# Attention kernel with two concatenated parts: reordered start-up (GpSimd work, weight and transposing loads, keep matmuls) and a halved last step

## Chip, cores, metric

One core of a Trainium2 chip. In the profile's lines PE is TensorE (matrix products), DVE VectorE, ACT ScalarE (the exponentials), POOL or Pool GpSimd and SP SyncE; a name with q, as ACTq, is that engine issuing a load or store. The granted clock is the share of full speed that the profile's records give for PE's clock; a keep matmul is one on zeros whose only use is to keep PE busy. The time of a run is device microseconds of that core; the span of a profile is about 2 us shorter than the time of the same run. A ratio between two kernels is the mean time of one kernel's runs over the mean time of the other's runs of the same rounds. The rounds of the experiments ran on four chips of the same kind, and the kernel before was run again in each of them; where medians of different rounds are compared, the text says so.

## The reference

Two attention blocks on sequences of 2048 rows, width 448, 16 heads of 28, both in bf16; their outputs are concatenated.

```python
# A: plain multi-head attention
qkv = x @ wqkv;  scores = q @ k.T * 28 ** -0.5
a = (softmax(scores) @ v) @ wo
# B: four segments of 512 rows, causal attention inside a segment, plus a memory
#    of the earlier segments (phi = elu + 1), gated by sigmoid(beta)
p = softmax(qs @ ks.T * scale + mask);  a_dot = p @ vs
a_mem = (phi(qs) @ M) / (phi(qs) @ z + 1e-6)
o = g * a_mem + (1 - g) * a_dot;  M += phi(ks).T @ vs;  z += phi(ks).sum()
b = o @ wo
return concatenate([a, b], -1)
```

## The kernel before

Names: P = 128, CW = 512 rows to a block, GW = 112 = four heads of 28, HP = 32 (a head padded to 32), D = 448. `xn` is the first block of A's input as rows, `xT` the input transposed, `wpad` the k or q weights with every head padded to 32 columns, `w["0"]` a small tile with the first four heads' weights, `w["A"]` the full weights of A (the profile calls it wstA).

```python
nc.sync.dma_start(out=xn[:], in_=Ax[0:CW, :]...)            # SP queue, 448 KB
load_w("0", A_wqkv, GW, D, GW, nc.scalar)                   # small k weights, ACT queue
load_w("0", A_wqkv, 0, 0, GW, nc.gpsimd)                    # small q weights, Pool queue
# ... Pool: memsets of wpad, vA, vB, woA, woB, phik, mblk, masks, one after the other ...
keep(11)                                                    # matmuls on zeros, while xn is on its way
# 16 transposes of xn on PE -> PSUM -> xT["A", 0, 0..3] (two copies by DVE, two by ACT)
for which in ("q", "k"):                                    # the padded copies, on DVE
    nc.vector.tensor_copy(out=wpad[which, "A"]...[:, :, 0:4, 0:DH], in_=w["0"]...)
nc.vector.memset(w["A"][KC // 2:KC // 2 + 1, 3, 0:2], 0.0)  # holds the next load until here
load_w("A", A_wqkv, 0, 0, 3 * D, nc.scalar)                 # 1008 KB + 168 KB, ACT queue
for r in (1, 2, 3):                                         # rows 512 to 2047, held until here
    for c in range(NKC):
        load_xT("A", Ax, r, c, nc.sync, hold if r == 1 and c == 0 else None)
# 8 matmuls: first projections of k and q -> kT by DVE, qT by ACT; 3 keep matmuls
```

`load_w` makes two loads: 384 rows in one, the last 64 rows in the other. After this comes a software pipeline of 395 units: three score matmuls into PSUM, one exponential over 128x1536 on ACT, three matmuls with v. Everything else on PE (projections, v, outputs) is put between the units as filler. v of the first four heads (`g_v0`) takes its weights from `w["A"]`.

After the last unit comes a chain for the last block:

```python
nc.vector.reciprocal(rc[:], pd[:])
nc.vector.tensor_copy(out=rb..., in_=rc...to_broadcast(...))   # 128x512
# 4 fp32 matmuls -> pb (128x512);  oT = o * pb on DVE;  4 output matmuls (t = 0..3)
# casts: t = 0, 2 on DVE, stored from SP; t = 1, 3 on ACT, stored from ACT
```

The softmax here doesn't subtract the row's maximum and nothing guards it: scores larger than these inputs give would overflow.

## Time and profile before

Median 586.03 us of four runs (585.21 to 587.72).

| stage of the profiled run (585.21 us) | us |
|---|---|
| start to first exponential | 16.14 |
| first exponential to end of the last | 554.02 |
| last exponential to end | 12.84 |

From the page: busy time of the engines as a share of the span, PE's granted clock in 40 slices (9 is 90% or more of full speed), and the group of exponentials (output and input, count, then busy us, mean ns, and after the bar idle us before them).

```profile
...
PE 519.6 (89%) x3869; PEld 172.4 (30%) x3912; DVE 200.4 (34%) x386; ACT 548.9 (94%) x427; POOL 21.2 (4%) x41
...
PEclk8899999999999999999999999999999999999999
...
L448 ACT ACTIVATE pt<-ps_s 128x1536 bf16<-128x1536 f32 x395 | 538.7, 1590 | 10.3 <-PE ps_s L444 5.4
...
```

ACT is 94% busy and nearly all of it is exponentials with 10.3 us of idle time before them in total: the middle is bound by ACT. Only the first two slices, up to about 29 us, show PE's clock below 90%. So the ramp and the tail are what can be shortened, and a microsecond won in the ramp moves the whole train of exponentials.

The timeline of the first 24 us (start, duration, engine, line, operation, how many; in brackets the idle time of the engine before it and what ended it):

```profile
...
6.77 0.97 POOL L132 MEMSET vB<- 128x1024 bf16 x1
...
7.13 0.74 DVE L274 COPY wpqA<-w 128x448 bf16<-128x448 bf16 x1
...
7.79 2.85 DVE L274 COPY wpkA<-w 128x448 bf16<-128x448 bf16 x1
...
8.62 1.90 POOL L161 MEMSET woA<- 128x1792 bf16 x1
...
10.79 1.01 PE L290 MATMUL ps_h<-xTA,wpkA 128*128 128x512 bf16 x2 [3.93 <-DVE wstA L281]
...
12.08 0.49 ACTq L110 DMA_DIRECT2D wstA<-in_A_wqkv_dram  x1
...
16.14 1.45 ACT L448 ACTIVATE pt<-ps_s 128x1536 bf16<-128x1536 f32 x1 [1.15 <-PE ps_s L435]
17.25 0.41 PE L224 MATMUL ps_v<-wstA,xTA 128*128 128x112 bf16 x5 [0.91 <-DMA wstA<-in_A_wqkv_dram]
...
18.03 2.79 ACT L448 ACTIVATE pt<-ps_s 128x1536 bf16<-128x1536 f32 x2 [0.44 <-PE ps_s L435]
...
21.89 3.02 ACT L448 ACTIVATE pt<-ps_s 128x1536 bf16<-128x1536 f32 x2 [1.07 <-PE ps_s L435]
...
```

The two padded copies on DVE have the same shape, but one lasts 0.74 and the other 2.85 us, while Pool's memsets run beside it (two of them, of vB and woA, are shown). The q copy ends at 7.87 us, and the k copy at 10.64 us. The first projection waits for them until 10.79 us. The second part of the full weight load is issued at 12.08 us, and PE waits for it in the middle of v (17.25 us). Then the second exponential is 0.44 us late, and the fourth 1.07 us.

By stage (busy us of each engine, then PE's clock, DMA share and GB/s):

```profile
...
core 0: us, PE busy (x) PEld busy (x) DVE busy (x) ACT busy (x) POOL busy (x), PEclk, DMA share, GB/s
0.00:16.14 16.14, 10.91 (x44) 4.20 (x45) 5.43 (x10) 3.15 (x6) 14.82 (x24) 0.79 0.64 154
16.14:21.89 5.75, 4.35 (x34) 1.57 (x32) 0.62 (x1) 4.24 (x3) 4.51 (x15) 0.77 1.13 156
21.89:570.20 548.31, 497.72 (x3756) 162.91 (x3797) 190.26 (x368) 540.48 (x417) 1.83 (x3) 1.00 0.15 37
570.20:583.00 12.80, 6.62 (x41) 3.67 (x40) 4.11 (x8) 1.06 (x2) 0.00 (x0) 0.98 0.16 54
...
```

The clock is 0.79 and 0.77 of full speed in the first two stages and 1.00 in the middle. (The DMA share exceeds 1 in this view, 1.13 in the second stage; nothing here rests on that column.) The tail in the timeline:

```profile
...
577.03 0.69 DVE L639 TENSOR_TENSOR oT<-osb,ps_b 128x512 bf16<-128x512 f32 x1 [1.33 <-PE ps_b L636]
...
577.78 0.93 PE L591 MATMUL ps_yl<-woA,oT 128*128 128x448 bf16 x4 [0.78 <-DVE oT L639]
...
579.31 0.36 ACTq L602 DMA_DIRECT2D out_dram<-y  x1
579.87 0.53 ACT L597 CAST y<-ps_yl 128x448 bf16<-128x448 f32 x1 [0.59 <-DVE y L599]
580.43 0.36 ACTq L602 DMA_DIRECT2D out_dram<-y  x1
```

The multiply over 128x512 takes 0.69 us, and only then come the four output matmuls. ACT's second cast starts 0.59 us after its first has ended, because ACT issues a store in between (the bracket names DVE, but that cast had ended at 579.53 us, and the store's issue ended at 579.67); the span ends 2.2 us after the last issue.

### The profile page before, as it was taken

What the parts mean: (1) busy time and instruction counts of PE and PEld (TensorE: products, weight loads), DVE (VectorE), ACT (ScalarE), POOL (GpSimd) and SP (SyncE); (2) the same over time, 40 slices, a digit from 0 to 9 for tenths busy, and PEclk for the clock granted to TensorE, in tenths of its full rate; (3) what the DMA queues carried; (4) which work ended last, traced back from release to release, by engine and by line L of the source; (5) the groups of instructions that cost most, each with busy time, mean ns of one, the idle gap of its engine ahead of it and who ended that gap; (6) DMA issues with size and microseconds to landing.
All of it is one profiled execution on the core that took longest, in us unless ns stands there. A gap on an engine that the chain in (4) does not pass through costs nothing.

```text
span 583.0 us, 9605 instructions
## 1 busy us (share of the span) xinstructions
PE 519.6 (89%) x3869; PEld 172.4 (30%) x3912; DVE 200.4 (34%) x386; ACT 548.9 (94%) x427; POOL 21.2 (4%) x41
## 2 busy tenths in 40 slices
PE   6999998898998998988898989989998898888995
PEld 2333322222222322332233332322322323323332
DVE  3123322222225233344533232233444355354213
ACT  1899999999999999999999999999999999998991
POOL 9300000000000000000000000000000000000000
PEclk8899999999999999999999999999999999999999
DMA  5900000000640000001103012021031031043101
GB/s 148 145 1 3 19 3 19 10 10 3 158 89 20 3 18 3 19 3 43 36 3 79 1 22 59 1 43 53 12 92 46 6 93 34 24 119 93 59 9 55
DMA packets 43091, 24.16 MB, mean 41 GB/s; under 512 B 30700, under 2 KB 36684, under 8 KB 43048
## 3 DMA queue, kind: packets, MB, share of 16 engines
q1 hardware_dynamic: 41304, 21.12, 14.9%
q0 software_dynamic: 496, 0.91, 1.0%
q10 hardware_dynamic: 1248, 1.53, 0.9%
q8 instruction: 30, 0.49, 0.4%
q14 instruction: 13, 0.11, 0.1%
HBM read 15.50 MB, written 4.37 MB: 34 GB/s over the span
## 4 chain that ended last, share of the span: by engine, by line
ACT 59%; PE 19%; issue 13%; DVE 3%; POOL 3%; DMA 1%; SPq 0%; ACTq 0%; DVEq 0%; POOLq 0%
ACT pt L448 56%; PE ps_s L435 4%; PE acc L480 4%; PE ps_proj L211 2%; PE ps_s L444 2%; PE ps_s L426 2%; ACT phq L504 1%; PE ps_y L591 1%; ACT ek L676 1%; DVE y L599 1%; DVE osb L535 1%; PE ps_mem L516 1%; PE ps_yl L591 1%; DMA bc<-d 1%; DVE osb L575 0%
## 5 line engine op out<-in xcount | busy, mean ns | idle before, releaser
L448 ACT ACTIVATE pt<-ps_s 128x1536 bf16<-128x1536 f32 x395 | 538.7, 1590 | 10.3 <-PE ps_s L444 5.4
L435 PE MATMUL ps_s<-qTA,kTA 32*128 32x512 bf16 x1024 | 135.7, 385 | 4.8 <-ACT pt L448 1.7
L480 PE MATMUL acc<-pt,vA 128*32 128x512 bf16 x1024 | 128.9, 391 | 0.5 <-POOL negi L179 0.5
L426 PE MATMUL ps_s<-warm,ident 128*128 128x512 bf16 (+5 forms) x352 | 98.3, 327 | 34.3 <-ACT pt L448 25.7
L435 PEld LDWEIGHTS <-kTA 32*128 32x128 bf16 x1024 | 34.7, 91 | 143.3 <-issue 141.9
L480 PEld LDWEIGHTS <-vA 128*32 128x32 bf16 x1024 | 32.3, 93 | 71.2 <-issue 68.6
L426 PEld LDWEIGHTS <-ident 128*128 128x128 bf16 x366 | 35.4, 97 | 52.8 <-issue 43.0
L535 DVE COPY osb<-acc 128x512 f32<-128x512 f32 x32 | 22.1, 692 | 55.3 <-PE acc L480 55.1
L599 DVE CAST y<-ps_y 128x448 bf16<-128x448 f32 x28 | 17.5, 624 | 50.2 <-PE ps_y L591 50.2
L435 PE MATMUL ps_s<-qTB,kTB 32*128 32x384 bf16 (+3 forms) x256 | 24.5, 301 | 1.4 <-ACT pt L448 0.8
L444 PE MATMUL ps_s<-tri,negi 128*128 128x128 bf16 x256 | 25.1, 222 | 0.0
L216 DVE CAST kTA<-ps_proj 128x512 bf16<-128x512 f32 x15 | 10.4, 691 | 38.5 <-PE ps_proj L211 35.4
L216 DVE CAST qTA<-ps_proj 128x512 bf16<-128x512 f32 x15 | 10.4, 691 | 33.5 <-PE ps_proj L211 33.5
L244 DVE CAST vB<-ps_v 128x448 bf16<-128x448 f32 x16 | 9.9, 620 | 29.5 <-PE ps_v L239 29.5
L211 PE MATMUL ps_proj<-xTB,wpkB 128*128 128x512 bf16 x56 | 18.3, 383 | 1.1 <-issue 0.6
L573 DVE TENSOR_TENSOR oT<-osb,bc 128x512 bf16<-128x512 f32 x19 | 13.0, 687 | 18.3 <-DMA bc<-d 18.2
L211 PE MATMUL ps_proj<-xTB,wpqB 128*128 128x512 bf16 x53 | 18.0, 385 | 1.5 <-DVE macc L700 0.8
L216 DVE CAST kTB<-ps_proj 128x512 bf16<-128x512 f32 x16 | 10.9, 684 | 24.1 <-PE ps_proj L211 24.1
L211 PE MATMUL ps_proj<-xTA,wpqA 128*128 128x512 bf16 x56 | 18.2, 384 | 1.0 <-issue 0.2
L211 PE MATMUL ps_proj<-xTA,wpkA 128*128 128x512 bf16 x54 | 18.3, 401 | 0.5
L239 PE MATMUL ps_v<-wstB,xTB 128*128 128x448 bf16 x64 | 18.7, 359 | 0.0
L444 PEld LDWEIGHTS <-negi 128*128 128x128 bf16 x256 | 14.7, 97 | 13.5 <-issue 13.5
(116 smaller groups left out, 329.9 us busy)
## 6 DMA issues: line engine op xcount, KB each, us to landing
bc<-d SPq DMA_DIRECT2D x48, 128.0 KB
bc<-d SPq DMA_DIRECT2D x76, 64.0 KB
out_dram<-y SPq DMA_DIRECT2D x30, 112.0 KB
wstA<-in_A_wqkv_dram ACTq DMA_DIRECT2D x1, 1008.0 KB
xn<-in_A_x_dram SPq DMA_DIRECT2D x1, 448.0 KB
woA<-in_A_wo_dram POOLq DMA_DIRECT2D x4, 98.0 KB, 3.6
woB<-in_B_wo_dram POOLq DMA_DIRECT2D x4, 98.0 KB, 5.8
wstB<-in_B_wq_dram SPq DMA_DIRECT2D x1, 336.0 KB
```

The source lines that it names most:

```text
L211: nc.tensor.matmul(ps[:], lhsT=wpad[which, side][:, c, g * P:(g + 1) * P], rhs=xc(side, sc, c)[:], start=(c == 0), stop=(c == NKC - 1))
L216: nc.vector.tensor_copy(out=dst[:], in_=ps[:])
L239: nc.tensor.matmul(ps[:, 0:n], lhsT=xc(side, t // 4, c)[:, (t % 4) * P:(t % 4 + 1) * P], rhs=w[side][:, c, 2 * D + h0 * DH:3 * D], start=( ...
L426: nc.tensor.matmul(ps[:, 0, 0:n], lhsT=ident[:], rhs=warm[:, 0:n], start=True, stop=True)
L435: nc.tensor.matmul(ps[:, i, o0:o0 + wd], lhsT=kT[side, g, t // 4][rows, (t % 4) * P:(t % 4 + 1) * P], rhs=qT[side, g, q0 // CW][rows, q0 % ...
L444: nc.tensor.matmul(ps[:, i, o0:o0 + P], lhsT=negi[:], rhs=tri[:], start=False, stop=True, skip_group_check=True)
L448: nc.scalar.activation(out=pt[:, 0:n, :], in_=ps[:, 0:n, :], func=ACT.Exp, scale=scale)
L480: nc.tensor.matmul(acc[key][j * HP:(j + 1) * HP, a0:a0 + wd], lhsT=v[side][:, t, h * HP:(h + 1) * HP], rhs=pt[:, i, c0:c0 + wd], start=fir ...
L535: nc.vector.tensor_copy(out=o[:, 0, :], in_=a[:])
L573: nc.vector.tensor_mul(oT[key][:], o[:, 0, :], bc[:, 0, :])
L591: nc.tensor.matmul(ps, lhsT=oT[side, g, s][:, t * P:(t + 1) * P], rhs=wo[side][:, g, :], start=(g == 0), stop=(g == G - 1))
L599: nc.vector.tensor_copy(out=y[:], in_=ps)
```

## The change

The intent: keep Pool off VectorE while the padded copies run, keep PE's clock up, let v and the later rows arrive earlier, and let the two halves of the last step overlap.

```diff
+    load_w("0", A_wqkv, 2 * GW, 2 * D, GW, nc.sync)     # small v weights, 98 KB, behind xn
...
+        if hold:
+            nc.vector.memset(t[0:1, 0, DH:HP], 0.0)     # vA: Pool's memset waits for DVE
...
     keep(11)
+    def hold(t):
+        nc.vector.tensor_copy(out=t[0:1, 0:2], in_=xn[0:1, 0, 0:2])   # was: memset after the copies
+    for r in (1, 2, 3): ... load_xT(...)                # moved up: held only until xn has landed
 # transposes, padded copies
+    v["A"] = vtile("vA", hold=True)                     # moved below the padded copies
 # ... rest of Pool's chain ...
-    load_w("A", A_wqkv, 0, 0, 3 * D, nc.scalar)
+    load_w("A", A_wqkv, 0, 0, 3 * D, nc.gpsimd)         # moved behind Pool's chain
+    keep(3)
...
     g_v0:  rhs=w["A"][:, c, 2 * D:2 * D + GW]  ->  rhs=w["0"][:, c, 2 * GW:3 * GW]
...
     # last block: broadcast, fp32 matmuls, multiply and output matmuls in two halves;
     # store of t = 1 from SP instead of ACT, so ACT issues only the store of t = 3
```

## The prediction

> **What bounds the kernel.** The page gives ACT 94% of a 583.0 us span; 395 exponentials (128x1536, 1.59 us mean) are 538.7 us, and idle time before them is only 10.3 us. The timeline shows the first exponential at 16.14 us, then gaps of 0.44 and 1.07 us, an unbroken train from 21.89 us, and the last one ending at 570.2 us. So there is a ramp of about 16 us, a saturated middle, and a tail of about 13 us. The change touches only ramp and tail; a microsecond won before the train starts should move everything behind it.
>
> **Ramp before.** The 128x448 copy into the padded k weights lasts 2.85 us (7.79 to 10.64), while the page's 128x1344 copy of the same kind lasts 0.50 us. Pool memsets run during all of it. [...] Meanwhile PE idles 3.9 us, its granted clock falls to 0.50 from 9.2 to 15.8 us, and the eight first projections and three keep matmuls run at 0.43 us each. Then v waits 0.91 us for the 1008 KB weight load, and the clock is 0.50 again from 19.3 to 22.7 us, which makes the 1.07 us gap.
>
> **What the change does there.**
> - vA's Pool memset waits for the k copy: I expect that copy at 0.25 to 0.5 us (estimate from the 0.50 us copy), so the first projection starts near 7.8 instead of 10.79 us: about 3 us.
> - Three more keep matmuls fill PE's idle time, so the clock should stay at 1.0 through the eight projections: 0.22 instead of 0.43 us each, about 1.7 us. [...]
> - The small v weight load (98 KB) lands by about 6 us, so the 0.91 us wait goes; transposing loads start near 5.6 instead of 10.9 us, early enough for the k projection of rows 512 on.
> - The full load moves behind Pool's chain (16.6 us long from vA's memset): issued near 25, landed near 31 us (estimate), wanted near 38 us. Free.
>
> First exponential near 11 us (saved about 5), with about 1.1 of the 1.5 us of early gaps gone. Ramp: 6 us.
>
> **Tail.** Timeline: reciprocal at 574.99, broadcast 0.43, eight fp32 matmuls, multiply 0.69, four output matmuls 0.93, casts to 580.40, last store issued 580.43, end 583.0. Halving lets the second half's matmuls run under the first half's multiply (about 0.35 us); sending t=1's store from SP takes 0.6 us of issue out from between ACT's two casts. Last store issued near 579.1: 1.3 us saved.
>
> **Sum.** 586.0 - 6.0 - 1.3 = 578.7; I take 579.0 us, 8 in 10 between 577.0 and 582.0. Faster by over 2%: 0.02; within 2%: 0.97; slower: 0.01.
>
> **What would show it.** Padded k copy under 0.6 us; projections at about 0.22 us with the clock at 1.0 between 6 and 10 us; first exponential at 10.5 to 12 us; idle after the first three exponentials under 0.6 us; no VectorE wait at the padded copies of the remaining heads; the middle unchanged (first to last exponential about 552.5 us against 554.0); last exponential to end about 11.4 us against 12.8.
>
> **What would make it wrong.** [...] PE is slow in the first projections (2 us less); transposed rows or VectorE evictions make new gaps in the train; a Pool chain later than thought starves the padded copies (slower); the tail is held by the last store's landing, so that only half its gain shows.

## The result

The changed kernel: median 577.94 us of 11 runs (576.23 to 579.1). Before, in the same rounds: 587.06 us. Ratio 0.984 (95%: 0.9812 to 0.9868). That is 1.6%, within the 2% that counts as the same, and clear of noise. The spread shrank from 8.4 to 2.9 us.

| stage, profiled runs | before | after |
|---|---|---|
| start to first exponential | 16.14 | 11.29 |
| first exponential to end of the last | 554.02 | 553.03 |
| last exponential to end | 12.84 | 12.18 |
| span | 583.0 | 576.5 |

The timeline of the changed kernel's first 24 us, the lines that answer to those of before:

```profile
...
7.69 0.27 DVE L240 COPY wpqA<-w 128x448 bf16<-128x448 bf16 x1
7.87 0.27 DVE L240 COPY wpkA<-w 128x448 bf16<-128x448 bf16 x1
...
8.22 0.95 POOL L135 MEMSET vA<- 128x1024 bf16 x1 [3.82 <-DVE vA L133]
...
8.29 0.59 PE L294 MATMUL ps_h<-xTA,wpkA 128*128 128x512 bf16 x2 [0.22 <-DVE vA L133]
...
9.58 0.59 PE L294 MATMUL ps_hq<-xTA,wpqA 128*128 128x512 bf16 x2
...
11.29 13.54 ACT L452 ACTIVATE pt<-ps_s 128x1536 bf16<-128x1536 f32 x10 [0.49 <-PE ps_s L439]
...
```

Both padded copies last 0.27 us, Pool's memset of vA comes after them, the projections follow each other at 0.215 us (two starts are 1.29 us apart over six matmuls), and from 11.29 us the exponentials run without a gap. By stage:

```profile
...
0.00:11.29 11.29, 9.68 (x47) 4.37 (x48) 2.46 (x10) 3.15 (x6) 6.81 (x15) 1.00 0.48 114
11.29:14.08 2.79, 2.37 (x27) 1.32 (x26) 0.62 (x1) 2.79 (x3) 2.73 (x3) 1.00 0.60 95
14.08:564.32 550.24, 500.08 (x3762) 163.04 (x3803) 189.96 (x368) 541.87 (x418) 13.00 (x27) 1.00 0.16 40
564.32:576.50 12.18, 6.68 (x41) 3.66 (x40) 4.39 (x10) 0.97 (x3) 0.00 (x0) 1.00 0.17 57
...
```

PE's clock reads 1.00 in all four stages. (It reads 1.00 in the first 6 us too, although the eleven keep matmuls there, from 1.37 to 6.03 us, take about 0.42 us each; the three added ones, from 7.26 us, follow each other at 0.215 us.) One short fall is hidden in the long one:

```profile
...
519.37 1.45 ACT L452 ACTIVATE pt<-ps_s 128x1536 bf16<-128x1536 f32 x1 [1.10 <-PE ps_s L439]
...
```

At 517 to 518 us PE waits 1.43 us for VectorE, from 518.7 to 522.1 us its clock is 0.50, and ACT loses 1.10 and then 0.63 us. In two later profiles without this fall of the clock (keep8_no3 and tail3q) ACT loses 0.90 and 0.80 us there in all. Not every run has the fall: of the twelve recorded runs of the changed kernel, the four with a mean clock of 1.000 took 577.3 us on average, the eight with 0.996 to 0.998 took 578.3. In the profiles of no_keep, tail_merge and keep8_early_x, with mean clocks of 0.997, 0.996 and 0.997, ACT loses 1.72 and 0.62, 1.47 and 0.62, and 1.70 and 0.51 us at the same place. So about 1 us of what is left of the spread goes with such a fall in the middle and not with the start, and a difference of 1 us between two of the later kernels says little. The tail:

```profile
...
560.59 13.46 SPq L606 DMA_DIRECT2D out_dram<-y  x7
...
571.24 1.00 PE L654 MATMUL ps_yl<-woA,oT 128*128 128x448 bf16 x4
...
572.28 0.97 ACT L601 CAST y<-ps_yl 128x448 bf16<-128x448 f32 x2 [7.95 <-PE ps_yl L654]
...
```

ACT's two casts now follow each other directly (0.97 us for both), and the output matmuls start while the second multiply is still running. But the last of SP's seven stores is issued only by 574.05 us (560.59 + 13.46), and the span ends 2.45 us after that. From last exponential to end, 0.66 us are won (spans are printed to 0.1 us, so about 0.7).

The profiles differ by 6.5 us, the medians by 9.1. The profiled run of the kernel before (585.21 us) lies 1.85 us below its median, that of the changed kernel (578.57 us) 0.63 us above its own; that makes up the difference. Experiment 1 shows what such luck of a run consists of.

### The profile page after: what moved, and what is told of

Same layout as the page of the kernel before. It is cut to its first block, busy times and chain, and to the rows that moved or that the text cites. A ratio compares the mean times of both kernels' runs of the same rounds, so it can differ in the third digit from the quotient of the medians.

```text
span 576.5 us, 9616 instructions
## 1 busy us (share of the span) xinstructions
PE 518.8 (90%) x3872; PEld 172.4 (30%) x3915; DVE 197.4 (34%) x388; ACT 548.8 (95%) x427; POOL 22.5 (4%) x43
## 4 chain that ended last, share of the span: by engine, by line
ACT 60%; PE 20%; issue 13%; DVE 4%; DMA 1%; SPq 0%; DVEq 0%; ACTq 0%
ACT pt L452 58%; PE ps_s L439 5%; PE acc L484 4%; PE ps_proj L170 2%; PE ps_s L448 2%; PE ps_s L430 2%; PE ps_y L595 1%; ACT phq L508 1%; ACT ek L691 1%; DVE y L603 1%; PE ps_h L218 1%; DVE osb L539 1%; PE ps_mem L520 1%; DMA bc<-d 1%; DVE osb L579 0%
## 5 line engine op out<-in xcount | busy, mean ns | idle before, releaser
L175 DVE CAST qTB<-ps_proj 128x512 bf16<-128x512 f32 x16 | 11.0, 687 | 21.4 <-PE ps_proj L170 21.4
```

The source lines that it names most:

```text
L175: nc.vector.tensor_copy(out=dst[:], in_=ps[:])
```

## The experiments

Every kernel gave correct results. The "stages" below are read from the profiled run of each kernel as in the tables above.

| kernel | median us (lowest to highest) | ratio to before (95%) | first exp. | first to last | last to end |
|---|---|---|---|---|---|
| before_again | 589.03 (586.37 to 590.66) | 1.0036 (0.9995 to 1.0076) | 15.34 | 558.71 | 12.85 |
| hold_only | 585.68 (583.89 to 586.72) | 0.9977 (0.9936 to 1.0017) | 14.21 | 557.42 | 12.87 |
| small_v_only | 583.52 (583.32 to 589.18) | 0.9954 (0.9925 to 0.9982) | 16.22 | 557.56 | 13.22 |
| clock_only | 590.12 (586.43 to 592.93) | 1.0021 (0.9967 to 1.0075) | 15.55 | 559.75 | 12.90 |
| no_hold | 582.35 (581.38 to 584.46) | 0.9929 (0.9893 to 0.9966) | 15.22 | 553.25 | 12.13 |
| late_x | 582.61 (581.74 to 583.65) | 0.9924 (0.9909 to 0.9938) | 11.30 | 556.72 | 12.18 |
| no_keep | 577.61 (576.5 to 580.34) | 0.9852 (0.9815 to 0.989) | 10.98 | 553.39 | 12.13 |
| old_tail | 578.66 (578.35 to 578.84) | 0.9852 (0.9839 to 0.9865) | 10.76 | 553.09 | 12.85 |
| tail3q | 578.93 (577.83 to 580.02) | 0.9858 (0.9841 to 0.9874) | 10.59 | 552.8 | 12.61 |
| tail_merge | 578.35 (577.62 to 580.74) | 0.9871 (0.9832 to 0.9909) | 10.98 | 553.12 | 12.7 |
| keep8_no3 | 576.55 (575.83 to 578.47) | 0.9837 (0.9804 to 0.9871) | 9.87 | 552.32 | 12.11 |
| keep8_early_x | 577.91 (577.07 to 579.1) | 0.9856 (0.9827 to 0.9886) | 10.31 | 553.5 | 12.09 |

The first four are the kernel before with at most one thing done to it; the others are the changed kernel with something undone or altered.

**1. The kernel before, once more (before_again).** No edit.

> The kernel before, run again to see what its spread (583 to 592 us) comes from. If it comes from the clock [...], the mean granted clock of its runs lies between about 0.985 and 0.995 and the slow runs are the ones with the low clock: a clock lower by 0.003 is about 3.4 us spent at half clock. If it comes from the loads, the time varies at an unchanged clock.

The first expectation held, as a correlation (the clocks of these six runs, 0.982 to 0.991, lie a little lower than expected). In all 50 runs of the kernel before that the experiments took with their clock, time and mean granted clock go together with a correlation of -0.82; the runs reach from 582.91 to 592.95 us, the clocks from 0.996 down to 0.978. But a correlation names no cause, and the profile shows that the load and the clock go together. The timeline of this run:

```profile
...
15.34 1.45 ACT L448 ACTIVATE pt<-ps_s 128x1536 bf16<-128x1536 f32 x1 [1.20 <-PE ps_s L435]
...
19.57 0.62 PE L224 MATMUL ps_v<-wstA,xTA 128*128 128x112 bf16 x5 [4.03 <-DMA wstA<-in_A_wqkv_dram]
...
20.79 2.85 ACT L448 ACTIVATE pt<-ps_s 128x1536 bf16<-128x1536 f32 x2 [4.00 <-PE ps_s L435]
...
25.01 1.45 ACT L448 ACTIVATE pt<-ps_s 128x1536 bf16<-128x1536 f32 x1 [1.37 <-PE ps_s L435]
...
27.06 1.45 ACT L448 ACTIVATE pt<-ps_s 128x1536 bf16<-128x1536 f32 x1 [0.60 <-PE ps_s L435]
...
29.16 12.20 ACT L448 ACTIVATE pt<-ps_s 128x1536 bf16<-128x1536 f32 x9 [0.65 <-PE ps_s L435]
...
```

The same wait of v for the full weights, 0.91 us in the profile that I had read, is 4.03 us here, and the second exponential comes at 20.79 instead of 18.03 us. The clock in this run:

```profile
...
15.00:18.50 3.50, 0.54 (x6) 0.21 (x4) 0.00 (x0) 1.45 (x1) 3.42 (x7) 0.98 1.23 115
...
19.50:24.00 4.50, 4.16 (x25) 1.70 (x24) 0.62 (x1) 2.85 (x2) 1.22 (x7) 0.50 1.23 232
24.00:28.30 4.30, 4.30 (x24) 1.37 (x24) 0.69 (x1) 2.69 (x2) 0.00 (x0) 0.50 0.60 114
...
```

PE idles almost 3 us of 15.0 to 18.5 us, and the clock is 0.50 from 18.5 us on. It stays there until about 28.8 us although PE is busy 8.46 of the 8.8 us from 19.5 to 28.3 us. While it does, each unit takes longer than an exponential (the exponentials at 25.01, 27.06 and 29.16 us start about 2.1 us apart and last 1.45 us), and three more gaps (1.37, 0.60, 0.65 us) open. The profile from which I predicted was one of the faster runs of its kernel.

**2. The hold on Pool alone (hold_only).** The kernel before, with this only:

```diff
-    v["A"] = vtile("vA")                    # before the padded copies
+    v["A"] = vtile("vA", hold=True)         # after them; Pool's memset waits for DVE
```

> Kernel before with nothing of the change but the order of Pool's work (the memset of vA waits for the padded copies). Theory ([...]the gain can only be collected with the small v weights): the k copy falls from 2.85 to about 0.27 us and the first projection starts near 8.3 us, but ACT still sits in its queue until the first part of the full weight load has landed (12.1 us) and v waits for the rest (17 us), so the first exponential comes near 13.5 us, the second not before about 17.5 us, and only 1 to 3 us of the 9 are won: about 584 to 586 us. Rival [...]: first exponential near 11.5 us, second 1.4 us later, about 579 to 580 us.

The first theory held, with the first exponential 0.7 us later than expected. The timeline:

```profile
...
7.72 0.27 DVE L236 COPY wpkA<-w 128x448 bf16<-128x448 bf16 x1
...
12.40 0.48 ACTq L110 DMA_DIRECT2D wstA<-in_A_wqkv_dram  x1
...
12.92 0.59 ACT L296 CAST qTA<-ps_hq 128x512 bf16<-128x512 f32 x1 [4.54 <-DMA wstA<-in_A_wqkv_dram]
...
16.07 0.63 PE L182 MATMUL ps_v<-wstA,xTA 128*128 128x112 bf16 x5 [1.50 <-DMA wstA<-in_A_wqkv_dram]
...
```

The k copy is down to 0.27 us. But the second part of the full load waits in ACT's queue until 12.40 us (in the profile of before, whose trace has the landings of both parts on one semaphore, the last of the first part's 16 landings is at 11.99 us and the second part is issued at 12.08), so ACT cannot copy q before 12.92 us, the first exponential is at 14.21 us, and PE then waits 1.50 us for v's weights. Of the 9 us only 1.8 are seen in the medians, and the interval of the ratio still includes no gain. PE's clock is 0.50 from about 13.2 to 23.5 us, after these waits have begun.

**3. The clock alone (clock_only).** The kernel before, with 14 more keep matmuls ahead of the first projections:

```diff
+    keep(14)
     hq = scp.tile([P, NB, CW], FP32, tag="sc", name="ps_hq")
```

> Kernel before with 14 more keep matmuls (about 3.0 us at full clock) in PE's idle time between the transposes and the first projection, nothing else. If the clock by itself is worth much: projections at 0.22 us, first exponential near 14.4 us, and the median 1.5 us or more below that of before. If it is worth little as long as v waits for the full weights: first exponential earlier by 1 to 2 us, but the second one still at 18 to 21 us and the median within 0.7 us of before.

The clock is 1.00 from 4 to 16 us (0.78 on average from 16 to 20, 0.50 from 20 to 24 us), and the projections ran at 0.22 us. No gain is seen: the first exponential is not earlier than in experiment 1 (15.55 against 15.34 us), and the median is 1.8 us above that of before in the same rounds. The interval of the ratio (0.9967 to 1.0075) leaves room for a gain of at most 0.3%.

```profile
...
13.93 0.50 ACTq L110 DMA_DIRECT2D wstA<-in_A_wqkv_dram  x1
14.47 0.59 ACT L294 CAST qTA<-ps_hq 128x512 bf16<-128x512 f32 x1 [7.00 <-DMA wstA<-in_A_wqkv_dram]
...
20.44 0.63 PE L224 MATMUL ps_v<-wstA,xTA 128*128 128x112 bf16 x5 [4.68 <-DMA wstA<-in_A_wqkv_dram]
...
```

ACT sits behind the second part of the full load until 13.93 us, and v waits 4.68 us for it. (The run also shows that this wait can be longer than the two that I had seen.) So in this run q's copy waited for the load, at a clock of 1.00. In the profile of before it had waited for PE (14.40 us, after ACT's queue was free at 12.57), whose projections ran at 0.43 us there, so the half clock did delay the start; but with the clock at 1.00 the next things to wait for, ACT's queue and v's weights, came as late or later in this run.

**4. The small v weights alone (small_v_only).** The kernel before, with these two lines (and the tile `w["0"]` widened to hold the v weights):

```diff
+    load_w("0", A_wqkv, 2 * GW, 2 * D, GW, nc.sync)
-    rhs=w["A"][:, c, 2 * D:2 * D + GW]
+    rhs=w["0"][:, c, 2 * GW:3 * GW]
```

> Kernel before with only the small v weight load (and v taken from it); Pool's order, the late transposing loads, the full weight load on ACT's queue and the tail stay. Theory (the wait of v for the full weights, 0.9 us in one profile of before and 4.0 us in the other, and the cold clock that follows it, make the part of the gain that I undersized, and the spread): the first exponential stays at 15 to 16 us, the wait before the second goes, the median is 2 to 4 us below that of before and the spread of the runs shrinks from 8 to under 4 us. Rival (that wait matters little): within 1 us of before, spread as before.

The theory held in size: 3.6 us in the medians (0.46% or 2.7 us by the ratio of the means). On the spread it is not shown: five of the six runs lie within 1.3 us of each other (583.32 to 584.55), but the sixth makes it 5.9 us, and the kernel before had only 2.8 us in the same rounds (586.06 to 588.87). The sixth, which was the profiled one, took 589.18 us; it shows what comes next. After the third exponential PE waits 1.49 and 0.17 us for transposed rows, and three score matmuls, which took 0.39 us at 16.85 us, take 0.61 us at 21.70, 23.97 and 26.29 us, as in experiment 1 at a clock of 0.50.

**5. The changed kernel without the hold (no_hold).**

```diff
-    v["A"] = vtile("vA", hold=True)
+    v["A"] = vtile("vA")
```

> Changed kernel with the hold on Pool's vA memset taken away, everything else kept. Theory [...]: the k copy is back near 2.9 us, PE idles 2 to 3 us before the first projection in spite of three keep matmuls, the clock falls to 0.5 and the first exponential comes at 14 to 16 us; 3.5 to 5 us slower than the changed kernel, about 582 us. Rival (keep matmuls and loads carry the gain): first exponential within 1 us of 11.3 us, within 1.5 us of 577.9.

The theory held. The timeline:

```profile
...
7.79 2.85 DVE L240 COPY wpkA<-w 128x448 bf16<-128x448 bf16 x1
...
10.79 0.59 PE L294 MATMUL ps_h<-xTA,wpkA 128*128 128x512 bf16 x2 [3.54 <-DVE wpkA L240]
...
```

The k copy is back at 2.85 us, the first projection at 10.79 us as before the change, and the three added keep matmuls do not help: the clock is 0.50 from about 11.9 to 15.3 us. From 15.22 us on the train has no gap. The median is 4.4 us above that of the changed kernel (different rounds; by the ratios to before, 0.993 against 0.984), and 4.7 us above that of experiment 7, which ran in the same rounds.

That the copy lasts 2.85 us again is not a speed. In all five profiles in which the copies stand beside Pool's memsets, the q copy starts at a different time (6.63 to 7.55 us) and ends at 7.87 or 7.88 us, and the k copy ends at 10.64 to 10.67 us; in before, before_again, clock_only and no_hold each ends 0.12 to 0.14 us after a memset has ended. So the length of a copy there is the time from its start to just after the end of a memset.

**6. The changed kernel with late transposing loads (late_x).**

```diff
-    for r in (1, 2, 3): ... load_xT(...)        # ahead of the transposes
+    for r in (1, 2, 3): ... load_xT(...)        # after the padded copies, held by a memset there
```

> Changed kernel with the twelve transposing loads held back again behind the padded copies (issued from about 8.2 instead of 4.9 us). Theory: the first exponential stays near 11.3 us, but the k projection of rows 512 on, wanted near 13.7 us, waits for its last slice; 0.5 to 2 us slower than the changed kernel. Rival (those loads have slack): same within 0.4 us, no wait of PE for a load.

Both expectations missed: it costs 4.7 us by the medians (different rounds; ratio to before 0.992 against 0.984). The first exponential is at 11.30 us as in the changed kernel and the first seven follow without a gap, but then:

```profile
...
20.74 0.38 PE L170 MATMUL ps_proj<-xTA,wpkA 128*128 128x512 bf16 x1 [1.22 <-DMA xTA<-in_A_x_dram]
...
23.26 0.38 PE L170 MATMUL ps_proj<-xTA,wpkA 128*128 128x512 bf16 x1 [2.14 <-DMA xTA<-in_A_x_dram]
...
24.07 1.45 ACT L452 ACTIVATE pt<-ps_s 128x1536 bf16<-128x1536 f32 x1 [3.26 <-PE ps_s L439]
...
```

SP issues the twelve loads over 16.6 us, one after the other, and the third block's slices come too late: PE waits 1.22 and 2.14 us, three score matmuls then take 0.61 us at 25.40 us against 0.39 us at 23.56 and 27.52 us, and ACT is idle for 3.26 us. In the changed kernel the first of these loads is issued at 4.93 instead of 8.21 us, and its slices come just in time: no wait shows there, but experiment 10, which moves the train forward by 1.4 us, finds one of 0.9 us.

**7. The changed kernel without the three added keep matmuls (no_keep).**

```diff
-    keep(3)
```

> Changed kernel without the three added keep matmuls. PE then idles about 0.9 us between the transposes and the first projection. Theory as I predicted (they keep the clock up): the clock falls to 0.5 in some runs and the first exponential comes 1 to 3 us later, 579 to 581 us. Rival (the gap is now too short for the clock to fall): projections still at 0.22 us each, first exponential at 11.3 us, time within 0.5 us of 577.9.

The rival was right. With the copies short, PE idles only 0.86 us before the projections, the clock stays at 1.00 there, they run at 0.215 us, and the time is the same (577.61 against 577.94 us, different rounds). One of the six runs took 580.34 us at a clock of 0.993, below any of the changed kernel's; for that run the first theory is not excluded.

**8. The changed kernel with the old tail (old_tail).** The last block's code is that of before; the rest is unchanged.

> Changed kernel with the old tail. In the profiles the time from the end of the last exponential to the end of the span is 12.8 us before and 12.2 us after, so the tail's part should be about 0.7 us here: last exponential to end 12.8 us, median near 578.5 us. My prediction's 1.3 us would give 13.5 us and 579.2 us.

Last exponential to end is 12.85 us against 12.18: the new tail is worth 0.67 us, not 1.3.

**9. What holds the new tail (tail3q, tail_merge).** Two edits of the last four stores:

```diff
 # tail3q
-                  nc.scalar if t == 3 else nc.sync)
+                  (nc.sync, nc.gpsimd, nc.sync, nc.scalar)[t])
 # tail_merge: t = 0, 2 cast into one tile and stored from SP; t = 1, 3 from ACT
+            (nc.scalar if i else nc.sync).dma_start(out=dst[:, i, :, :], in_=ys[i][:])
```

> Changed kernel, but the store of t=1 goes from Pool's queue, so that SP has two of the last stores to issue instead of three. Theory (the tail is held by SP issuing three stores in a row after the casts have ended): last exponential to end falls from 12.2 to about 11.8 us. Rival (the landing of Pool's own store, or of the last, holds it): 12.2 us or longer.

> Changed kernel with the last four stores merged into two, one from SP and one from ACT, each issued after its second cast. If SP's three stores in a row hold the tail, last exponential to end falls from 12.2 to about 11.8 us; if a store of twice the size lands later by as much, it stays at 12.2.

Neither brought 11.8 us; with Pool's store it came as the rival said. With Pool the last issue ends 9.36 us after the last exponential instead of 9.73 us, as wanted, but the span ends 3.25 us after it instead of 2.45 us (12.61 us in all). With two stores of 224 KB instead of four of 112 KB the last issue ends after 9.41 us, and the span 3.29 us after that (12.7 us in all). So taking issue time away is not enough: the landing grew by as much or more. What exactly is waited for in those 2.45 us these runs do not show.

**10. A shorter start (keep8_no3, keep8_early_x).** In the changed kernel xn has landed at 4.75 us, but PE is busy with its keep matmuls until 6.03 us.

```diff
 # keep8_no3
-    keep(11)
+    keep(8)
-    keep(3)
 # keep8_early_x: the same, and
-            load_xT("A", Ax, r, c, nc.sync, hold if r == 1 and c == 0 else None)
+            load_xT("A", Ax, r, c, nc.sync)
```

> Changed kernel with 8 instead of 11 keep matmuls at the start and without the three added ones, so that the first transposes can start when their rows have landed (4.75 us) and not when PE is through with its keep matmuls (6.0 us). If the start is held by PE: first exponential near 10.2 us instead of 11.0 to 11.3. If the transposed loads pace the ramp behind it (the last experiment gave them 0.5 to 1.7 us of slack), part of that comes back as a wait of PE for a load near 20 us; median 0 to 1 us below 577.9.

> As keep8_no3, and the transposing loads no longer wait for the first rows: SP issues them from about 2.4 us. If their own pace is what holds the rows, all later rows come 2 to 2.5 us sooner, no wait for them is left, and the median is 0.5 to 1.5 us below that of the changed kernel. Rival: they take the DMA engines from the first rows and weights, which land later than 4.75 us, and the first exponential moves past 11 us.

For keep8_no3 both halves of the expectation came true:

```profile
...
9.87 10.85 ACT L451 ACTIVATE pt<-ps_s 128x1536 bf16<-128x1536 f32 x8 [0.49 <-PE ps_s L438]
...
21.11 20.26 ACT L451 ACTIVATE pt<-ps_s 128x1536 bf16<-128x1536 f32 x15 [0.38 <-PE ps_s L438]
...
```

The transposes start at 4.75 us and the first exponential comes at 9.87 us; before the ninth one ACT then waits 0.38 us, because PE waits 0.9 us for a transposed slice. With a median of 576.55 us this is the fastest kernel, below both the kernel before and the changed one. It was not run in the same rounds as the changed kernel, 1.4 us between medians of different rounds is small, and by the ratios to before (0.9837 against 0.984) the two can't be told apart. In keep8_early_x the twelve loads are issued from 2.43 us and no wait for them is left, but the q weights land later (the q copy waits for them until 6.71 us), the first exponential is at 10.31 us, and the median is 577.91 us. The rival's mechanism is there, but it explains 0.44 us of the 1.36 between the two medians; this profile also has the short fall of the clock near 518 us, which that of keep8_no3 has not, and a middle that is 1.2 us longer.

## Why the prediction was right, and which terms were mis-sized

The time (579.0 predicted, 577.94 measured, range 577 to 582) and the class (within 2%) were right.

- *The k copy.* Right: 0.27 us (0.25 to 0.5 predicted). Experiments 2 and 5 show that Pool's work beside it makes the difference: without the hold the same copy is back at 2.85 us, and ends 0.13 us after a memset of Pool has ended.
- *The first projection near 7.8 us.* It was 8.29 us; the first transpose ran at 6.03 us because of the eleven keep matmuls, which experiment 10 shortens.
- *Three keep matmuls hold the clock, 1.7 us.* The clock stayed at 1.00 and the eight projections did run at 0.215 us, but not because of these matmuls (experiment 7): with the copies short, PE idled for 0.86 us without them, and the clock did not fall there in the profiled run (1.00 up to 34 us). And a clock of 1.00 alone brought no gain that could be seen in the kernel before (experiment 3). The step that failed is the attribution: I gave the 1.7 us to the keep matmuls, and added it as if it stood in series with everything else.
- *The v wait, 0.91 us, and the early gaps.* Mis-sized. I took them from one profile of one of the faster runs. In another run of the same kernel the wait is 4.03 us and four gaps of 6.6 us in all follow the first exponential (4.00 + 1.37 + 0.60 + 0.65). The small v weights alone bring 3.6 us in the medians.
- *Transposing loads "early enough".* Right, but I gave them no value. Without this part 4.7 of the 9 us are lost again (experiment 6).
- *The full load behind Pool's chain is free.* Right: issued at 24.83 and 25.61 us, landed 5.8 and 5.5 us later, wanted at 36.80 us, no wait. Moving it also clears ACT's queue, which held q's copy in experiments 2 and 3; no run undoes this move alone, so its share of the gain is not shown.
- *First exponential near 11 us, no early gaps, middle 552.5 us.* 11.29 us, none, and 553.03 us.
- *The tail, 1.3 us.* Mis-sized: 0.66 us in the profiles, 0.67 in experiment 8. The casts ended 1.3 us earlier, as predicted, but three stores in a row on SP and the landing took half of it back.

That the time came within 1.1 us of the forecast is in part luck. Between the two profiled runs the ramp gained 5.84 us (6.0 predicted) and the tail 0.66 (1.3 predicted). The medians gained more than the profiled runs, because the profile that I had read was of one of the faster runs, and this made up for the tail.

The parts do not add up because they are gates side by side. The train can start and keep going only when the padded copies, ACT's queue, v's weights and each block of transposed rows are all there. Opening one shows the next: the hold alone gives 1.8 us (not clear of noise), the small v weights alone 3.6 us, yet taking the hold out of the finished kernel costs 4.4 us and taking the early rows out costs 4.7 us.

## What to carry to other kernels

At the start of a kernel with one saturated engine, list every arrival that its first dozen instructions need, with the time of each; only the latest one counts, and the value of opening one gate is read from the next gate, not from the wait that vanishes. Before you cost a change from one profile, look at the spread of the runs and where that profile lies in it: here the wait for one and the same load was 0.9 us in one run and 4 us in another. A low clock on PE after a wait may be the trace of the wait, and then in turn stretch what follows, as in experiment 1 (0.50 from 18.5 us, inside a wait of 4.03 us, and exponentials 2.1 us apart after it); test what it is worth by raising the clock alone. And when an operation ends at the same time in every run, whenever it started (the k copy beside Pool's memsets at 10.64 to 10.67 us, the q copy at 7.87 or 7.88), look for what it is waiting for.

## What these runs show of the clock, the copies and the loads

- In the second profile of the kernel before (experiment 1), the clock stayed at 0.50 from 18.5 to about 28.8 us, although PE was busy (as the profile counts it) 8.46 of the 8.8 us from 19.5 to 28.3 us.
- In the first profile it fell to 0.50 at 19.3 us, after 3.4 us in which PE was busy for 2.0 us. It was the same in the changed kernel at 518.7 us, after 3.4 us with PE busy for 2.0.
- In the first profile the k copy did not get in between two of Pool's memsets (one ended at 9.02 us, the next had started at 8.62) and ended only 0.12 us after the second: 2.85 us against 0.27 us without them. The q copy beside these memsets lasted from 0.32 us (small_v_only) to 1.25 us (clock_only), by when it started. So it is not a ratio of lengths that carries from one of these profiles to another; the time until a memset is through does.
- Merging the last stores was no gain: two stores of 224 KB ended the span 3.29 us after the last issue, four of 112 KB 2.45 us after it.
- In the profile of before, the landings of both parts of the full load are on one semaphore, and the second part is issued 0.09 us after the last landing of the first (12.08 us against 11.99). In the five profiles in which ACT issues this load the second part is issued at 12.08 to 13.93 us, 5.0 to 7.5 us after the first; in experiments 2 and 3 ACT's copy of q sat behind it.
